# Layer 2 of a fused attention and MLP kernel: differences on another engine, sums in PSUM chains, attention at other times

## The chip, the cores and the metric

One core of a Trainium2 chip runs the whole program. The metric is the device time of one execution in microseconds (us). A profile is one separate execution, recorded instruction by instruction. The engines are TensorE (PE; its weight loads are listed apart as PEld), VectorE (DVE), ScalarE (ACT) and GpSimd (POOL); SyncE (SP) issues the DMAs. Each runs its instructions in the order in which they stand.

## The reference, cut to what matters

Attention with a per-head decay `lam`, then an MLP. q, k, v are (4, 8, 768, 64), in 12 blocks of 64; the MLP is 512 to 2048 to 512 over 3072 tokens, all float32.

```python
for b in range(nb):                       # 12 blocks of 64
    intra = einsum('bhic,bhjc->bhij', qb, kb) * Dmask      # Dmask[i, j] = lam ** (i - j), i >= j
    intra = einsum('bhij,bhjd->bhid', intra, vb)
    inter = einsum('bhid,bhde->bhie', qb * lam_pow, kv_state)
    out[:, :, sl] = intra + inter
    kv_state = lam_block * kv_state + einsum('bhsd,bhse->bhde', kb * rev_pow, vb)
h = x @ w_in                              # x: the attention's output, tokens x 512
g = maximum(h, 0) + log1p(exp(-abs(h)))   # softplus
return g @ w_out
```

## The kernel before, in words

Every float32 matrix product of the MLP is three float32r products: an operand is split in a high half (a rounding copy on ScalarE) and a low half (a subtraction on VectorE), and high x high, high x low and low x high are summed in PSUM. The 3072 tokens are six chunks of 512 (4 batch rows x 128 positions).

- Chunks 0 and 1 run a plain ("classic") MLP. For each of 16 blocks of 128 hidden rows there are 12 matmuls of layer 1 (`mlp1`, into a PSUM bank `h`), a softplus (`chain_act`), the split (`chain_hi`, `chain_lo`) and 12 matmuls of layer 2 (`mlp2`, into four banks `o`). There are two `h` banks; attention's output `z` uses them as well.
- Chunks 2 and 3 (group q=1) and chunks 4 and 5 (q=2) run with 7 block products in place of 8 (a Strassen-Winograd scheme) in both layers. Layer 1 (`l1`) makes four blocks 11, 12, 21, 22 of the softplus in SBUF. Layer 2 (`l2`, n = 0 to 6, each n four pieces jp, each piece 12 matmuls) needs differences of these blocks: `l2_minus` makes them in place on GpSimd, 16 instructions of 128x1024 in each group. `l2_split` splits a piece into the tile `gb`, `l2_products` multiplies it with the weights `wb`, `l2_end` takes a finished product out of PSUM into the sums U, P, V, R, and `l2_store` writes a block of 512 x 256 to HBM.
- The weight sums for the 7 products are made on GpSimd beside the classic stage (`prepare`: tiles `cs`, split into `sk`, stored to HBM as `w1d` and `w2d`).
- Attention of chunk c is four units g (`burst`: `outs` of one unit and `scores` of the next on TensorE; masks, decays and states on VectorE and ScalarE), put between the MLP's matmuls. `x_copy` takes `z` out of PSUM, `x_minus` and `x_block` make the seven split operands `xb` of layer 1.

From classic block 16 of the sequence on, the order is made at build time by `Plan`: each operation has an engine, an assumed duration, its buffers and a due time. Where several could start on an engine, the earliest due goes first. On the chip only the resulting order on each engine holds, with semaphores for data and buffers. 22 slots `b8` of 8 KB in a partition hold the loads and the split operands.

Lines used below: `chain_act` 589, `chain_hi` 593, `chain_lo` 597, `mlp1` 608, `mlp2` 622, `outs` 509, `scores` 478 and 482, `prepare` 866 to 898, `load_unit` 916, keys' decay 926, masks 946, copy of a state 955, query decay 971, `x_copy` 981, `x_block` 993 and 996, `x_minus` 1004, `l1_products` 1075, `l1_sum` 1122, `l2_minus` 1190, `l2_split` 1199 and 1202, `l2_products` 1217, `l2_end` 1235 and 1237, `l2_store` 1247.

Of the kernel before, what the change touches and what calls it, by code (L numbers as in the profile page):

```python
# [18 lines left out]
NP = H // 2  # L19
# [4 lines left out]
LAG = 4  # L24


class Plan:
# [57 lines left out]
    def order(self):  # L85
# [25 lines left out]
        while done < len(ops):  # L111
# [81 lines left out]
def decay_attention_softplus_ffn(  # L193
# [660 lines left out]
    def prepare(which, j):  # L854
        e, o = 2 * j, 2 * j + 1
        pairs = [divmod(w_order.index((f, which)), 2) for f in (e, o)]
        due = clock
# [34 lines left out]
        add("DVE", dve(1024), lo, [*four, (*sk, 0)], [(*sk, 1)], due=due + 7)  # L892
# [18 lines left out]
    def load_unit(g, due):  # L911
        if g < 2 * NP + 2:
            return

        def load():
            nc.sync.dma_start(out=unit(g), in_=att[g // NP, g % NP])

        add("SP", 0.06, load, [], u_keys(g, "q", "k0", "k1", "kt2", "kt3", "v"), [("b8", ("U", g))], size=1.05, due=due, behind=bursts.get(g - 2))
# [22 lines left out]
    def after_scores(g, due):  # L941
# [25 lines left out]
        for n, r in ((1, hi), (0, lo)):  # L967
# [4 lines left out]
            add("DVE", 0.69, decay, [("t", g)], u_keys(g, "q"), due=due)  # L972
# [14 lines left out]
    def x_block(q, n, c, p, due):  # L987
# [11 lines left out]
        add("DVE", dve(1024), low, [*of, (*key, 0)], [(*key, 1)], due=due)  # L999

    def x_minus(q, to, x, y, due):
# [52 lines left out]
    def l1_load(q, j):  # L1054
        for n, (a, b) in enumerate(((0, 4), (4, 7))):
            def load(n=n, a=a, b=b):
# [4 lines left out]
                due=clock - 7, behind=l1_ops.get((q, j - 2) if j > 1 else (q, -1)),  # L1061
# [126 lines left out]
    def l2_minus(q, jp, to, x, y, due):  # L1188
        def minus():
            nc.gpsimd.tensor_sub(out=l_pair(q, to, jp), in0=l_pair(q, x, jp), in1=l_pair(q, y, jp))  # L1190
        add("POOL", pool(1024), minus, lks(q, x, jp) + lks(q, y, jp), lks(q, to, jp), due=due)

    def l2_split(q, n, jp):
        blk = blocks[n]
# [9 lines left out]
        add("ACT", act(1024), high, lks(q, blk, jp), [(*key, 0)], [("b8", key)], due=clock - 4, behind=l2_ops[-4] if len(l2_ops) > 3 else l1_ops[q, 6])  # L1204
        add("DVE", dve(1024), low, [*lks(q, blk, jp), (*key, 0)], [(*key, 1)], due=clock - 2)

    def l2_products(q, n, jp):
        key = ("G2", q, n, jp)

        def run():  # L1210
            if jp == 0:
                E2[q, n] = [obank(f"e{q}_{n}_{m}") for m in range(2)]
            w = W2[q, n, jp // 2]
            for k in range(2):
                for m in range(2):
                    for r, (a, b) in enumerate(((0, 0), (1, 0), (0, 1))):
                        nc.tensor.matmul(  # L1217
                            E2[q, n][m], lhsT=w[:, 2 * (jp % 2) + k, a, m * 128 : (m + 1) * 128], rhs=G2[key][:, b, k],
                            start=jp == 0 and k == 0 and r == 0, stop=jp == 3 and k == 1 and r == 2,
                        )  # L1220

        return ffn(
            R12, run, [(*key, 0), (*key, 1), ("W2", q, n, jp // 2, 0)], [("E2", q, n, m, 0) for m in range(2)],
            [("o", ("E2", q, n, m)) for m in range(2)] if jp == 0 else (),
        )

    def l2_end(q, name, n, of=None, op=ALU.add, due=1.0):

        for m in range(2):
            def run(m=m):  # L1230
                if name not in OB or OB[name][0] != q:
                    OB[name] = q, t4([128, 2, 512], F32, f"{name}{q}")
                to = OB[name][1][:, m]
                if of is None:
                    nc.scalar.copy(out=to, in_=E2[q, n][m])
                else:
                    nc.vector.tensor_tensor(out=to, in0=OB[of][1][:, m], in1=E2[q, n][m], op=op)  # L1237
            key = ("OB", q, name)
            add(
                "ACT" if of is None else "DVE", 0.69, run,  # L1240
                [("E2", q, n, m, 0), *([] if of is None else [("OB", q, of, m)])], [(*key, m)],
                [("b4", key)] if m == 0 and of != name else (), due=clock + due,
            )

    def l2_store(q, name, c, dh):
        def run():
            nc.sync.dma_start(
                out=out[c, dh * 256 : (dh + 1) * 256].rearrange("(m q) i -> q m i", m=2), in_=OB[name][1]
            )
# [121 lines left out]
```

## Time and profile before

| | |
|---|---|
| Time, median of 3 runs | 568.33 us (567.51 to 569.15) |
| Time of the profiled execution | 567.39 us |
| Its span, first to last instruction | 565.6 us |
| TensorE busy | 549.1 us (97%) |
| VectorE busy | 426.5 us (75%) |
| ScalarE busy | 288.7 us (51%) |
| GpSimd busy | 215.8 us (38%) |

A row of the timeline gives the start, the time from the start of the first to the end of the last instruction of its run, engine, line, operation, output<-inputs, shape and count; in square brackets is the idle time ahead of it and who ended it. A row of waits gives the sum, the number and the longest. Matmuls are pipelined: one 128x512 matmul is listed at 393 ns, while a run of them advances by 227 ns each, so runs are read by their starts. The MLP of the classic chunks fills the first 226 us, group 1 the stretch to 409 us, group 2 the rest; layer 2 of group 1 starts at 316.7 us, that of group 2 at 485.1 us.

### The profile page before, as it was taken

Reading aid. Unit: us, or ns where it says so; the run is one execution under the profiler, and the core shown is the slowest. Engines: PE = TensorE matmul, PEld = TensorE weight load, DVE = VectorE, ACT = ScalarE, POOL = GpSimd, SP = SyncE. Lnnn points to the kernel's source line nnn. Section 1 sums busy time; section 2 is a strip of 40 time slices with the busy share of each in tenths; the row PEclk is TensorE's granted clock in tenths of the full one; section 3 lists DMA queues with packets and bytes.
Section 4 is the critical chain, followed back from the end, with each engine's and each line's share of the span. In section 5 each row is a group of like instructions: output and inputs, shape, how many; then the busy total and the mean of one; then the engine's idle time right before and its main releaser. Section 6 shows DMA issues by size and latency. Waiting matters only on the chain. (4 is left out here: it accounts for less than half of the span.)

```text
span 565.6 us, 10346 instructions
## 1 busy us (share of the span) xinstructions
PE 549.1 (97%) x4275; PEld 449.6 (79%) x4275; DVE 426.5 (75%) x498; ACT 288.7 (51%) x420; POOL 215.8 (38%) x138
## 2 busy tenths in 40 slices
PE   8999999999999999799999999998999999999996
PEld 6888888888888878578788878876888888888885
DVE  8999999969267678985666999999533336779763
ACT  5998975475445456545446653355023234474300
POOL 1000000475445468675440979920000006869100
PEclk9999999999999999999999999999999999999999
DMA  8999699838734449279966957462798332528502
GB/s 309 399 407 407 232 373 368 279 150 280 280 149 149 150 159 378 116 269 349 403 203 229 374 220 261 149 225 75 270 412 339 131 124 100 222 90 319 224 0 111
DMA packets 37919, 136.97 MB, mean 242 GB/s; under 512 B 3186, under 2 KB 11378, under 8 KB 29042
## 3 DMA queue, kind: packets, MB, share of 16 engines
q1 hardware_dynamic: 37872, 136.33, 64.8%
q8 instruction: 33, 0.54, 0.4%
q14 instruction: 12, 0.10, 0.0%
q10 hardware_dynamic: 2, 0.00, 0.0%
HBM read 100.66 MB, written 35.65 MB: 241 GB/s over the span
## 5 line engine op out<-in xcount | busy, mean ns | idle before, releaser
L1217 PE MATMUL e<-gb,wb 128*128 128x512 f32 x672 | 156.4, 393 | 2.8 <-DVE gb L1202 2.8
L1190 POOL TENSOR_TENSOR l<-l,l 128x1024 f32<-128x1024 f32 x32 | 104.2, 3281 | 126.2 <-DVE gb L1202 125.6
L1217 PEld LDWEIGHTS e<-gb,wb 128*128 128x128 f32 x672 | 126.7, 189 | 30.3 <-DVE gb L1202 3.6
L866 POOL TENSOR_TENSOR cs<-w 128x512 f32<-128x512 f32 x32 | 48.4, 1534 | 180.3 <-PE h L608 105.3
L1202 DVE TENSOR_TENSOR gb<-l,gb 128x1024 fp32r<-128x1024 f32 x56 | 97.3, 1774 | 6.7 <-ACT gb L1199 6.6
L608 PE MATMUL h<-x,w 128*128 128x512 f32 x384 | 92.2, 392 | 1.3 <-ACT xs L981 1.3
L622 PE MATMUL o<-w,g 128*128 128x512 f32 x384 | 92.4, 392 | 0.0
L608 PEld LDWEIGHTS h<-x,w 128*128 128x128 f32 x384 | 71.5, 188 | 16.8 <-ACT xs L981 1.5
L622 PEld LDWEIGHTS o<-w,g 128*128 128x128 f32 x384 | 71.5, 188 | 15.2
L1075 PE MATMUL B<-xb,wa 128*128 128x512 f32 x288 | 71.9, 392 | 3.9 <-DVE xb L996 2.6
L1199 ACT CAST gb<-l 128x1024 fp32r<-128x1024 f32 x56 | 56.5, 1049 | 26.4 <-PE e L1217 10.1
L1075 PEld LDWEIGHTS B<-xb,wa 128*128 128x128 f32 x288 | 53.6, 188 | 16.5 <-DVE xb L996 3.4
L880 POOL TENSOR_TENSOR cs<-cs 128x256 f32<-128x256 f32 x64 | 61.8, 980 | 2.5
L1104 ACT ACTIVATE l<-l 128x512 f32<-128x512 f32 x48 | 30.2, 631 | 44.6 <-DVE l L1122 44.5
L1075 PE MATMUL D<-xb,wa 128*128 128x512 f32 x192 | 49.0, 391 | 0.0
L1075 PE MATMUL A<-xb,wa 128*128 128x512 f32 x192 | 48.9, 390 | 0.0
L597 DVE TENSOR_TENSOR g<-l,g 128x512 fp32r<-128x512 f32 x32 | 28.8, 899 | 17.6 <-ACT g L593 17.3
L1075 PEld LDWEIGHTS A<-xb,wa 128*128 128x128 f32 x192 | 35.9, 188 | 7.7 <-DMA wa<-w1d 0.2
L1075 PEld LDWEIGHTS D<-xb,wa 128*128 128x128 f32 x192 | 35.9, 188 | 7.5
L589 ACT ACTIVATE l<-h 128x512 f32<-128x512 f32 x32 | 19.1, 597 | 36.1 <-PE h L608 28.7
L971 DVE TENSOR_TENSOR att<-att,lp 64x512 f32<-64x512 f32 x32 | 31.6, 989 | 0.5
L926 ACT ACTIVATE att<-att,rp 64x256 f32<-64x256 f32 x56 | 27.9, 505 | 7.2 <-DMA att<-in_att 6.5
(111 smaller groups left out, 621.9 us busy)
## 6 DMA issues: line engine op xcount, KB each, us to landing
wb<-w2d SPq DMA_DIRECT2D x28, 1024.0 KB, 5.7
att<-in_att SPq DMA_DIRECT2D x17, 1024.0 KB, 7.3
raw<-in_wts SPq DMA_DIRECT2D x32, 512.0 KB, 10.1
wa<-w1d SPq DMA_DIRECT2D x16, 1024.0 KB, 8.1
wa<-w1d SPq DMA_DIRECT2D x16, 768.0 KB, 9.2
w1d<-sk SPq DMA_DIRECT2D x8, 1024.0 KB, 4.8
w2d<-sk SPq DMA_DIRECT2D x8, 1024.0 KB, 5.5
w2d<-w SPq DMA_DIRECT2D x24, 256.0 KB, 4.4
```

The costliest lines, as they stand in the source:

```text
L597: nc.vector.tensor_sub(out=g[:, 1, :], in0=l_tiles.pop(s), in1=g[:, 0, :])
L608: nc.tensor.matmul(h_tiles[s], lhsT=w[:, i, cs], rhs=x[:, j, :], start=p == 0 and n == 0, stop=p == NP - 1 and n == 2,)
L622: nc.tensor.matmul(o_tiles[c][b], lhsT=g[:, i, b * 128 : (b + 1) * 128], rhs=w[:, j], start=f == 0 and n == 0, stop=f == NF - 1 and n == 2,)
L866: nc.gpsimd.tensor_add(out=T8[cs][:, 2 * n : 2 * n + 2].rearrange("q h e -> q (h e)"), in0=w[:, 0], in1=w[:, 1])
L880: nc.gpsimd.tensor_tensor(out=t[:, to], in0=t[:, x], in1=t[:, y], op=op)
L971: nc.vector.tensor_mul(out=q, in0=q, in1=w[r])
L1075: nc.tensor.matmul(AB[q, j, to], lhsT=w[:, a, k * 128 : (k + 1) * 128], rhs=x[:, b, k], start=start and k == 0 and m == 0, stop=k == 1 and ...
L1104: nc.scalar.activation(l, l if of is None else AB[(q, j, of)], AF.Softplus)
L1190: nc.gpsimd.tensor_sub(out=l_pair(q, to, jp), in0=l_pair(q, x, jp), in1=l_pair(q, y, jp))
L1199: nc.scalar.copy(out=G2[key][:, 0], in_=l_pair(q, blk, jp))
L1202: nc.vector.tensor_sub(out=G2[key][:, 1], in0=l_pair(q, blk, jp), in1=G2[key][:, 0])
L1217: nc.tensor.matmul(E2[q, n][m], lhsT=w[:, 2 * (jp % 2) + k, a, m * 128 : (m + 1) * 128], rhs=G2[key][:, b, k], start=jp == 0 and k == 0 an ...
```

## The change

- Layer 2's differences are made on VectorE (`nc.vector.tensor_sub`), and block 11 is changed twice in place of 22; the products run in the order of the table `order2`.
- Products that belong to one sum stay in PSUM: products 0 and 1 add up in the banks X, 4 and 2 in Y, and 5, 3 and 6 in X2 (`chains`). The sums are taken out when a chain or a prefix of it is done (`sums`): 10 VectorE additions and 4 ScalarE copies in a group, for 18 and 2. Each piece's 12 matmuls are two operations of 6, one for each half m of the output rows; each half is stored by itself (256 KB), eight stores in a group for four. `stores` names the output block of each.
- In the planned part the classic softplus is written in place into its PSUM bank, and both halves of the split read it there; the bank is free after the low half.
- The due times become a table `LEAD`: copies of `z` are due 20 us earlier, weight sums 2.7 us (w_in) and 5.6 us (w_out) earlier, splits 7 us earlier, attention's bursts start at other times and distances.

```diff
-            nc.gpsimd.tensor_sub(out=l_pair(q, to, jp), in0=l_pair(q, x, jp), in1=l_pair(q, y, jp))
-        add("POOL", pool(1024), minus, lks(q, x, jp) + lks(q, y, jp), lks(q, to, jp), due=due)
+            nc.vector.tensor_sub(out=l_pair(q, to, jp), in0=l_pair(q, x, jp), in1=l_pair(q, y, jp))
+        add("DVE", dve(1024), minus, lks(q, x, jp) + lks(q, y, jp), lks(q, to, jp), due=due, kind="two")
...
+        def soften():
+            l_tiles[s] = h_tiles.pop(s)
+            nc.scalar.activation(l_tiles[s], l_tiles[s], AF.Softplus)
+        add("ACT", 0.6, soften, [], [("h", s)], due=due)
+        add("ACT", 0.62, lambda: chain_hi(s), [("h", s)], [("g", s, 0)], [("b4", ("g", s))], due=due)
+        add("DVE", 0.69, lambda: chain_lo(s), [("h", s), ("g", s, 0)], [("g", s, 1), ("g", s)], due=due)
...
-    blocks = ("11", "21", "22", "12", "11", "22", "21")
+    order2 = ((0, "11"), (4, "11"), (1, "21"), (2, "22"), (5, "11"), (3, "12"), (6, "21"))
...
+    chains = {0: "X", 4: "Y", 1: "X", 2: "Y", 5: "X2", 3: "X2", 6: "X2"}
...
+        begins = w_n in (0, 4, 5)
+                    nc.tensor.matmul(
+                        E2[q, to, m], lhsT=w[:, 2 * (jp % 2) + k, a, m * 128 : (m + 1) * 128], rhs=G2[key][:, b, k],
+                        start=begins and jp == 0 and k == 0 and r == 0, stop=jp == 3 and k == 1 and r == 2,
...
+            nc.sync.dma_start(out=out[c, dh * 256 + m * 128 : dh * 256 + (m + 1) * 128], in_=OB[q, name][:, m])
+        add("SP", 0.06, run, [("OB", q, name, m)], [], size=0.262, due=clock + 3)
+    sums = {0: [("U", "X", None)], 4: [("D", "Y", "U")], 1: [("P", "X", None)], 2: [], 5: [("V", "X2", "U"), ("V", "Y", "V")], 3: [("D", "X2", "D")], 6: [("U", "X2", "U")]}
+    stores = {1: ("P", 0, 0), 5: ("V", 1, 0), 3: ("D", 1, 1), 6: ("U", 0, 1)}
...
-            attention(3, [clock + 7.5 * n for n in range(5)])
+            attention(3, [clock + LEAD["att3"] + LEAD["step3"] * n for n in range(5)])
...
-                attention(2 * q + 3, [clock + 10 * n for n in range(5)])
+                attention(2 * q + 3, [clock + LEAD["att5"] + LEAD["step5"] * n for n in range(5)])
```

VectorE in layer 2 of group 1 (gb1_n_jp: the split of piece jp of the n-th product; l1_11, l1_21, l1_22: blocks of the softplus; U1, P1, D1: sums; att20: an attention unit), before:

```order
L1202 TENSOR_TENSOR gb1_1_3_3479<-l1_21_1_3192,gb1_1_3_3479 128x1024
L1202 TENSOR_TENSOR gb1_2_0_3517<-l1_22_0_2628,gb1_2_0_3517 128x1024
L1202 TENSOR_TENSOR gb1_2_1_3534<-l1_22_0_2628,gb1_2_1_3534 128x1024
L1202 TENSOR_TENSOR gb1_2_2_3554<-l1_22_1_3062,gb1_2_2_3554 128x1024
L1237 TENSOR_TENSOR P1_3600<-U1_3475,e1_1_0_3481 128x512
L1237 TENSOR_TENSOR P1_3600<-U1_3475,e1_1_1_3482 128x512
L1202 TENSOR_TENSOR gb1_2_3_3602<-l1_22_1_3062,gb1_2_3_3602 128x1024
```

The same part of VectorE's order now:

```order
L1210 TENSOR_TENSOR gb1_2_3_3460<-l1_21_1_3054,gb1_2_3_3460 128x1024
L1198 TENSOR_TENSOR l1_11_0_2617<-l1_22_0_2628,l1_11_0_2617 128x1024
L1249 TENSOR_TENSOR D1_3485<-e1_Y_0_3414,U1_3412 128x512
L1210 TENSOR_TENSOR gb1_3_0_3476<-l1_22_0_2628,gb1_3_0_3476 128x1024
L1249 TENSOR_TENSOR D1_3485<-e1_Y_1_3426,U1_3412 128x512
L1210 TENSOR_TENSOR gb1_3_1_3496<-l1_22_0_2628,gb1_3_1_3496 128x1024
```

The differences (L1198) now stand among the splits; they were in GpSimd's order before.

ScalarE late in the classic stage (att14: the unit whose scores w14 are next; z12, z13: attention outputs in `h` banks; h28 to h30, l30: classic blocks; sk: weight sums), before:

```order
L885 CAST sk1_2_2169<-cs1_2_2168 128x4x256
L955 COPY att14_2094<-st_14_1795 64x512
L981 COPY xs3_2278<-z12_2096 128x512
L981 COPY xs3_2278<-z13_2215 128x512
L589 ACTIVATE l30_2317<-h30_2282 128x512
```

The same part now:

```order
L963 COPY att13_1893<-st_13_1595 64x512
L989 COPY xs3_2151<-z12_2078 128x512
L835 ACTIVATE h28_2129<-h28_2129 128x512
L598 CAST g28_2174<-h28_2129 128x512
L1001 CAST xb1_1_2179<-xs2_1656 128x1024
L893 CAST sk0_4_2147<-cs0_4_2146 128x4x256
L934 ACTIVATE att14_2169<-att14_2169,rp1_110 64x4x64 x4
L835 ACTIVATE h29_2182<-h29_2182 128x512
L598 CAST g29_2269<-h29_2182 128x512
L989 COPY xs3_2151<-z13_2219 128x512
L963 COPY att14_2169<-st_14_1774 64x512
L835 ACTIVATE h30_2272<-h30_2272 128x512
```

The copies of z12 and z13 moved ahead of att14's copy; a weight sum and att14's key decays stand ahead of h29.

TensorE's last matmuls (e2_6_m and e2_X2_m: the two halves m of the last sum), before:

```order
L1217 MATMUL e2_6_1_5037<-gb2_6_2_5033,wb2_6_1_5018 128x512 x3
L1217 MATMUL e2_6_0_5036<-gb2_6_3_5051,wb2_6_1_5018 128x512 x3
L1217 MATMUL e2_6_1_5037<-gb2_6_3_5051,wb2_6_1_5018 128x512 x3
L1217 MATMUL e2_6_0_5036<-gb2_6_3_5051,wb2_6_1_5018 128x512 x3
L1217 MATMUL e2_6_1_5037<-gb2_6_3_5051,wb2_6_1_5018 128x512 x3
```

And now:

```order
L1229 MATMUL e2_X2_1_4889<-gb2_6_1_4930,wb2_6_0_4928 128x512 x6
L1229 MATMUL e2_X2_0_4881<-gb2_6_2_4947,wb2_6_1_4965 128x512 x6
L1229 MATMUL e2_X2_1_4889<-gb2_6_2_4947,wb2_6_1_4965 128x512 x6
L1229 MATMUL e2_X2_0_4881<-gb2_6_3_4967,wb2_6_1_4965 128x512 x6
L1229 MATMUL e2_X2_1_4889<-gb2_6_3_4967,wb2_6_1_4965 128x512 x6
```

Half 0 is done 6 matmuls ahead of the end, where it was done 3 ahead.

## Rows read from the trace of the kernel before

**Rows 1.** The page: busy time, share of the span, instructions of each engine

```profile
PE 549.1 (97%) x4275; PEld 449.6 (79%) x4275; DVE 426.5 (75%) x498; ACT 288.7 (51%) x420; POOL 215.8 (38%) x138
```

**Rows 2.** Waits of PE: who waited for whom, us, times, longest

```profile
PE e L1217 <- DVE gb L1202: 2.8, 2, 2.3
PE B L1075 <- DVE xb L996: 2.6, 2, 2.1
PE h L608 <- ACT xs L981: 1.3, 1, 1.3
...
PE B L1075 <- ACT xb L993: 1.1, 1, 1.1
...
PE z L509 <- DVE att L971: 1.0, 1, 1.0
```

**Rows 3.** Windows: length, PE, PEld, DVE, ACT, POOL busy (count), PE clock, DMA

```profile
394.00:398.00 4.00, 4.00 (x11) 3.14 (x12) 3.82 (x4) 0.00 (x0) 0.00 (x0) 0.57 0.00 0
```

**Rows 4.** Chain that ended last: start us, us, engine, tile, line, count

```profile
316.67 2.75 PE e L1217 x12
...
393.87 15.05 PE e L1217 x58
...
485.08 75.49 PE e L1217 x333
...
560.60 1.37 DVE U L1237 x2
```

**Rows 5.** Timeline of DVE, and then POOL, in layer 2 of group 1

```profile
321.36 9.73 DVE L1202 TENSOR_TENSOR gb<-l,gb 128x1024 fp32r<-128x1024 f32 x3 [0.28 <-ACT gb L1199]
...
347.50 1.41 DVE L946 TENSOR_TENSOR att<-w,mask 64x512 f32<-64x512 f32 x2
...
375.33 0.69 DVE L971 TENSOR_TENSOR att<-att,lp 64x512 f32<-64x512 f32 x1
...
378.86 3.48 DVE L1202 TENSOR_TENSOR gb<-l,gb 128x1024 fp32r<-128x1024 f32 x3
...
339.13 31.61 POOL L1190 TENSOR_TENSOR l<-l,l 128x1024 f32<-128x1024 f32 x8 [2.96 <-DVE gb L1202]
```

**Rows 6.** Groups by line: count, busy us, mean ns, idle before

```profile
L1190 POOL TENSOR_TENSOR l<-l,l 128x1024 f32<-128x1024 f32 x32 | 104.2, 3281 | 126.2 <-DVE gb L1202 125.6
L1202 DVE TENSOR_TENSOR gb<-l,gb 128x1024 fp32r<-128x1024 f32 x56 | 97.3, 1774 | 6.7 <-ACT gb L1199 6.6
```

**Rows 7.** Timeline of ACT at the end of the classic stage

```profile
201.27 0.62 ACT L955 COPY att<-st 64x512 f32<-64x512 f32 x1 [2.17 <-PE w L482]
201.90 1.07 ACT L981 COPY xs<-z 128x512 f32<-128x512 f32 x2
```

**Rows 8.** Timeline of PE, ACT, DVE and POOL where layer 1 of group 1 begins

```profile
218.79 1.15 PE L509 MATMUL z<-att 128*64 128x64 f32 x32
...
221.20 0.59 ACT L981 COPY xs<-z 128x512 f32<-128x512 f32 x1
...
221.81 2.13 DVE L1004 TENSOR_TENSOR xs<-xs 128x1024 f32<-128x1024 f32 x1 [1.35 <-ACT xs L981]
...
230.73 1.21 DVE L996 TENSOR_TENSOR xb<-xs,xb 128x1024 fp32r<-128x1024 f32 x1
...
222.94 5.66 POOL L880 TENSOR_TENSOR cs<-cs 128x256 f32<-128x256 f32 x4
```

**Rows 9.** Timeline of ACT, DVE and PE around classic block 20

```profile
137.71 0.60 ACT L589 ACTIVATE l<-h 128x512 f32<-128x512 f32 x1 [2.60 <-PE h L608]
138.34 0.62 ACT L593 CAST g<-l 128x512 fp32r<-128x512 f32 x1
...
139.78 0.68 DVE L597 TENSOR_TENSOR g<-l,g 128x512 fp32r<-128x512 f32 x1
...
140.23 2.88 PE L608 MATMUL h<-x,w 128*128 128x512 f32 x12
```

**Rows 10.** Line 916, the loads of attention's units

```profile
DMA to landing us min/median/max: 4.7/7.5/11.5
```

More of the change, by code (lines that the diff above doesn't have):

```diff
@@ L856, in prepare @@
         pairs = [divmod(w_order.index((f, which)), 2) for f in (e, o)]
-        due = clock
+        due = clock + LEAD["prepare"] + which * LEAD["prepare2"]
         tag = f"{which}_{j}"
@@ L891, in prepare @@
         prepared.append(len(plan.ops))
-        add("DVE", dve(1024), lo, [*four, (*sk, 0)], [(*sk, 1)], due=due + 7)
+        add("DVE", dve(1024), lo, [*four, (*sk, 0)], [(*sk, 1)], due=due + 7, kind="two")
         if which == 0:
@@ L971, in decay @@
                 nc.vector.tensor_mul(out=q, in0=q, in1=w[r])
-            add("DVE", 0.69, decay, [("t", g)], u_keys(g, "q"), due=due)
+            add("DVE", 0.69, decay, [("t", g)], u_keys(g, "q"), due=due, kind="two")
     def x_copy(g, due):
@@ L998, in x_block @@
         add("ACT", act(1024), high, of, [(*key, 0)], [("b8", key)], due=due)
-        add("DVE", dve(1024), low, [*of, (*key, 0)], [(*key, 1)], due=due)
+        add("DVE", dve(1024), low, [*of, (*key, 0)], [(*key, 1)], due=due, kind="two")
     def x_minus(q, to, x, y, due):
@@ L1202, in low @@
             nc.vector.tensor_sub(out=G2[key][:, 1], in0=l_pair(q, blk, jp), in1=G2[key][:, 0])
-        add("ACT", act(1024), high, lks(q, blk, jp), [(*key, 0)], [("b8", key)], due=clock - 4, behind=l2_ops[-4] if len(l2_ops) > 3 else l1_ops[q, 6])
-        add("DVE", dve(1024), low, [*lks(q, blk, jp), (*key, 0)], [(*key, 1)], due=clock - 2)
-    def l2_products(q, n, jp):
+        add("ACT", act(1024), high, lks(q, blk, jp), [(*key, 0)], [("b8", key)], due=clock - LEAD["split"], behind=l2_ops[-LEAD["split_depth"]] if len(l2_ops) >= LEAD["split_depth"] else l1_ops[q, LEAD["split_from"]])
@@ L1208, in l2_products @@
+        add("DVE", dve(1024), low, [*lks(q, blk, jp), (*key, 0)], [(*key, 1)], kind="two", due=clock - LEAD["split"] + 2)
+    chains = {0: "X", 4: "Y", 1: "X", 2: "Y", 5: "X2", 3: "X2", 6: "X2"}
+    def l2_products(q, n, jp, m):
         key = ("G2", q, n, jp)
+        w_n = order2[n][0]
+        to = chains[w_n]
+        begins = w_n in (0, 4, 5)
         def run():
-            if jp == 0:
-                E2[q, n] = [obank(f"e{q}_{n}_{m}") for m in range(2)]
+            if jp == 0 and begins:
+                E2[q, to, m] = obank(f"e{q}_{to}_{m}")
@@ L1245, in l2_store, with l2_end @@
[L1245 to L1250 removed]
+            R6, run, [(*key, 0), (*key, 1), ("W2", q, n, jp // 2, 0)], [("E2", q, to, m)],
+            [("o", ("E2", q, to, m))] if jp == 0 and begins else (),
+        )
+    def l2_end(q, name, chain_, m, of=None, ahead=1.0):
+        def run():
+            if (q, name) not in OB:
+                OB[q, name] = t4([128, 2, 512], F32, f"{name}{q}")
+            to = OB[q, name][:, m]
+            if of is None:
+                nc.scalar.copy(out=to, in_=E2[q, chain_, m])
+            else:
+                nc.vector.tensor_add(out=to, in0=E2[q, chain_, m], in1=OB[q, of][:, m])
+        key = ("OB", q, name)
+        add(
+            "ACT" if of is None else "DVE", 0.6 if of is None else 0.69, run,
+            [("E2", q, chain_, m), *([] if of is None else [("OB", q, of, m)])], [(*key, m)],
+            [("b4", key)] if m == 0 and of != name else (), due=clock + ahead,
+        )
@@ L1318, in decay_attention_softplus_ffn @@
             if q < NCH // 2 - 1 and j == 0:
-                attention(2 * q + 2, [clock + 14 * n for n in range(5)])
+                attention(2 * q + 2, [clock + LEAD["att4"] + LEAD["step4"] * n for n in range(5)])
         for n in range(7):
```

106 lines of the change are left out of this document (36 added, 70 removed).

## The prediction, on record before the changed kernel ran

> **What bounds the kernel now.** I read the page's first part, then TensorE's waits, then the windows around the longest of them, then the other engines' timelines there. TensorE is busy for 549.1 of 565.6 us [rows 1], so work taken off another engine gives time back only where TensorE stands and waits for it. The change leaves every matmul in place, with its shape. What can be won is therefore a short list: TensorE's waits once the planned part runs, the time lost after a wait at a lower clock, and the end.
>
> The waits add up to 8.8 us [rows 2], apart from those of the start, which the change doesn't touch. The reader is to see where they are: 2.8 us for the split `gb` and 1.0 for an attention decay are in layer 2 of group 1, where VectorE has no idle time to speak of; 1.3 us is classic block 30, waiting for a copy of `z`; 2.6 and 1.1 us are the start of layer 1 of group 1, waiting for the operand `xb`. Group 2 has none: 333 matmuls run there in 75.49 us, 0.2267 us each [rows 4].
>
> [...]
>
> **Layer 2's differences on VectorE.** GpSimd's 32 instructions of 3.28 us [rows 6] go and 32 of VectorE come. The price is read where GpSimd is idle: three splits of the same form in 3.48 us, 1.16 each [rows 5]. While GpSimd works they take 3.24 each (9.73 for three), and 1.77 on the mean of all 56 [rows 5, 6]. A mask multiplication that reads PSUM keeps to 0.70 in the middle of GpSimd's run (1.41 for two) [rows 5], so it is the instructions with two SBUF inputs that are held up.
>
> [...]
>
> In layer 2 of group 1 VectorE then has 28 splits and 16 differences at 1.16, 51.0 us; 10 additions at 0.68 (1.37 for two [rows 4]), 6.8; five attention blocks of 3.5 us (375.33 to 378.86 [rows 5]), 17.7; and 11 differences and splits of `xs` at 1.16, 12.8: 88.3 us. TensorE has from 316.67 to 393.87 + 15.05 = 408.92 us [rows 4], 92.25 us, less the waits 3.8 and the clock's 1.9: 86.5 us. So VectorE is as loaded as TensorE. But six of these instructions (7.0 us) now stand ahead of layer 2's first matmul, in a part of layer 1 where VectorE has room, which leaves 81.3. By the order each split then comes 5 us or more ahead of its matmuls; closest is the last operand of group 2's layer 1, about 2 us ahead. The 3.8 us of waits and the 1.9 us of clock go: 5.7 us. Bounds: nothing gained if VectorE is slowed by something else than GpSimd (a rival below), and no gain above 5.7.
>
> In group 2, 44 x 1.16 + 6.8 = 58 us of VectorE stand against 76 of TensorE. Nothing waits there before, nor after.
>
> **Chains in PSUM.** Eight VectorE additions fewer and two ScalarE copies more in each group are counted above. The matmuls alternate by runs of 6 for 3, in four banks as before; layer 1 runs by 6 too. No price.
>
> **The end.** Today two additions, 1.37 us, follow the last matmul [rows 4], and then a store of 512 KB; the span ends at 565.6, 3.6 us after the second addition. Now half 0 is ready 6 matmuls (1.36 us) before the end, so one addition of 0.68 and a store of 256 KB are left. The addition saves 0.7. The smaller store saves between 0 (all of the 3.6 fixed) and 1.8 (none of it); I take 0.6, nearer to the fixed cost, since the store is alone at the end. Together 1.3.
>
> **Classic softplus in PSUM, copies of z.** Block 30 waits because the copies of two `z` (1.07 us) stand behind a copy that waits 2.2 us for the next scores [rows 7]. Now they stand ahead of it: 1.3 us go. In exchange an `h` bank is free only after both halves of the split, 1.3 us later than now (the softplus is 0.60; the halves add 0.62 and 0.68 [rows 9]). The tightest place is block 21, which takes block 20's bank: softplus from 137.71, low half 139.78 to 140.46, and block 21 starts at 140.23 [rows 9]. VectorE reaches that low half some 0.5 us earlier now, since block 19's no longer meets GpSimd; a wait of 0 to 0.5 us remains. A softplus written to PSUM isn't in the trace; one that reads PSUM takes 0.60 [rows 9], and I take the same.
>
> **Earlier weight sums and attention.** `prepare` moves up, and its VectorE halves stand ahead of low halves that free a bank (ahead of h29's, for one), behind GpSimd's sums and, on ScalarE, behind key decays that wait for a load. SP takes some attention loads later in its queue: unit 11 behind two weight stores. A unit's load lands 4.7 to 11.5 us after its issue, 7.5 on the median [rows 10]; in the order I find 1 to 3 us of room at a median load (units 14, 18 and 23), so a slow one costs up to 2.5 each. For all of this and block 21 together: 0 to 5 us; I take 1.7.
>
> **Layer 1's start.** After the last `z` of chunk 3 (218.79 + 1.15) comes its copy, done at 221.79, then VectorE's chain from 221.81 to 231.94 [rows 8]. TensorE is 3.2 us late for it, and 0.5 once more for the last operand. Now the copy is due earlier, but behind four key decays and a weight sum on ScalarE: the chain starts 0 to 1.1 us sooner, and GpSimd is still beside it. The 0.5 should go, since that operand moved up. I take 2.3 us left of 3.7, so 1.4 saved; bounds 0 and 3.7.
>
> **Sum.** 5.7 + 1.3 + 1.3 + 1.4 - 1.7 = 8.0 us saved. The profiled execution took 567.39, which gives 559.4; the median of the runs is 0.94 above that execution, so 560.3. I say 560.2.
>
> **Rivals.**
> 1. *The start of layer 1 comes free as well and nothing new waits.* The copy of `z` and the chain would have to gain 3 us; for it speaks the earlier due time, against it GpSimd's sums beside the chain [rows 8]. 560.2 - 1.7 - 2.3 = 556.2.
> 2. *Banks and loads take the gain back.* Held 1.3 us longer, `h` banks make TensorE wait where one is reused at once, at four places or so (5.2 us more than I count); low halves behind late weight sums do the same. For it: block 21's room of nearly nothing [rows 9] and loads up to 11.5 us [rows 10]. Against: most reuses have 5 us or more. 560.2 + 5.2 = 565.4.
> 3. *VectorE becomes the bound in layer 2 of group 1* (slower than before). If the differences and splits stayed at 1.77 us [rows 6] with GpSimd idle, 44 x 0.61 = 26.8 us come on top; VectorE would need 81.3 + 26.8 = 108.1 against 86.5, 21.6 late. Gone too would be the 5.7: 568.3 - 2.3 + 21.6 = 587.6. From a mean of about 1.45 us on (room of 5.2 plus the gain of 8.1, over 44) the change loses. Against it: 1.16 with GpSimd idle [rows 5].
>
> **How the numbers follow.** Forecast 0.66 (its own range 557.5 to 563.5, from the bounds 0 to 5 of the new waits and 0 to 3.7 at layer 1's start), rival 1 0.10, rival 2 0.16, rival 3 0.08. The range 556.3 to 565.2 takes in the first, nearly all of rival 1 and half of rival 2. A measurement here can tell 0.3%, 1.7 us: faster means below 566.6. Forecast, rival 1 and two thirds of rival 2 lie there: 0.87. Within 0.3% lies the rest of rival 2: 0.05. Slower is rival 3: 0.08.
>
> **What would show it right or wrong.** In layer 2 VectorE's `gb` and difference rows should be near 1.16 us, TensorE's list of waits should hold no `gb` line, and no window should show a clock below 1.00 between 300 and 420 us. The line for `xb` should stay, at 2 to 3 us. After the last matmul one addition of 0.68 should stand. GpSimd should end near 290 us. It would be wrong if new lines appear: `h` waiting for VectorE's split (the held banks), scores waiting for ScalarE's key decay or a load (late units), `gb` waiting at more than 1.3 us an instruction (rival 3).

## The result and the profile after

The changed kernel takes 560.50 us (median of 4 runs, 558.73 to 561.86) against 568.74 us (567.51 to 570.11) in the same comparison: ratio 0.9853, interval 0.9816 to 0.9889. Measured a second time it took 560.42 us (558.85 to 560.85), ratio 0.9841, interval 0.9819 to 0.9863. The forecast was 560.2.

The page's first line of the kernel after, and then its list of TensorE's waits from 20 to 560 us (us, times, longest), answer to [rows 1, 2]:

```profile
PE 549.3 (98%) x4275; PEld 450.9 (81%) x4275; DVE 412.6 (74%) x514; ACT 291.4 (52%) x424; POOL 109.7 (20%) x106
```

```profile
PE B L1083 <- DVE xb L1004: 2.5, 1, 2.5
PE z L514 <- DVE att L979: 0.9, 1, 0.9
PE B L1083 <- DVE l L1130: 0.5, 1, 0.5
```

TensorE does the same work. The lines for `gb` and `h` are gone, that for `xb` stayed. The attention decay that TensorE waits for is another one (at 218.97 us, where it was at 378.99), and the wait of 0.5 for a sum of layer 1 is new. GpSimd lost its half, and VectorE is less busy than before although 32 instructions came to it and only 16 short ones left: the differences no longer hold up its splits, which take 1.22 us on the mean of all 56 for 1.77 [rows 6]. The groups by line from 310 to 410 us (count, busy us, mean ns, idle before) and VectorE's timeline in layer 2 of group 1 answer to [rows 5, 6]:

```profile
L1210 DVE TENSOR_TENSOR gb<-l,gb 128x1024 fp32r<-128x1024 f32 x27 | 32.4, 1218 | 1.7 <-ACT gb L1207 1.7
L1198 DVE TENSOR_TENSOR l<-l,l 128x1024 f32<-128x1024 f32 x16 | 19.2, 1217 | 0.0
```

```profile
326.69 4.65 DVE L1210 TENSOR_TENSOR gb<-l,gb 128x1024 fp32r<-128x1024 f32 x4
...
341.00 2.35 DVE L1198 TENSOR_TENSOR l<-l,l 128x1024 f32<-128x1024 f32 x2
```

One instruction is listed at 1.22 us; four in a row take 4.65, 1.16 each, the price of the prediction.

Where the time went is read from the starts of the stages' first matmuls, in the profiled executions (us):

| stretch | before | after | second profile of after |
|---|---|---|---|
| to group 1's layer 1 | 225.44 | 225.51 | 225.38 |
| group 1, layer 1 | 91.07 | 91.28 | 90.49 |
| group 1, layer 2 | 92.25 | 87.14 | 87.12 |
| group 2, layer 1 | 76.16 | 76.16 | 76.16 |
| group 2, layer 2, to the end of the span | 80.68 | 80.01 | 79.95 |

One attention output `z` (32 matmuls, 1.08 us) moved from layer 1 to layer 2 of group 1: 128 of them stood in each stretch, now 96 and 160. Like for like, layer 2 of group 1 gained 6.2 us and layer 1 lost 1.3 (0.5 in the second profile).

The loss is at layer 1's start. Windows of the kernel after (length, busy us and count of PE, PEld, DVE, ACT, POOL, granted clock, DMA share, GB/s), with the whole of 300 to 400 us for [rows 3]:

```profile
230.00:232.00 2.00, 0.67 (x2) 0.57 (x3) 2.00 (x3) 0.76 (x2) 0.64 (x1) 0.66 0.01 4
232.00:234.00 2.00, 2.00 (x6) 1.58 (x5) 2.00 (x5) 0.41 (x1) 2.00 (x2) 0.50 0.31 121
234.00:236.00 2.00, 2.00 (x6) 1.55 (x5) 0.39 (x1) 0.64 (x1) 1.92 (x3) 0.50 1.02 384
236.00:238.00 2.00, 2.00 (x7) 1.52 (x7) 2.00 (x2) 0.00 (x0) 1.92 (x3) 0.63 1.05 298
...
300.00:400.00 100.00, 100.00 (x832) 82.33 (x831) 89.10 (x102) 54.01 (x70) 0.00 (x0) 1.00 0.62 232
```

In layer 2 of group 1 TensorE is busy all the time, at a granted clock of 1.00. At layer 1's start the granted clock was 0.50 in the windows from 232 to 236 us, and 0.66 and 0.63 in those beside them. The timelines of PE, DVE and POOL there answer to [rows 8]:

```profile
231.34 2.07 PE L1083 MATMUL B<-xb,wa 128*128 128x512 f32 x4 [2.54 <-DVE xb L1004]
233.21 2.76 PE L1083 MATMUL D<-xb,wa 128*128 128x512 f32 x6
235.77 2.34 PE L1083 MATMUL A<-xb,wa 128*128 128x512 f32 x6
237.95 1.55 PE L1083 MATMUL B<-xb,wa 128*128 128x512 f32 x6
...
221.07 2.31 DVE L1012 TENSOR_TENSOR xs<-xs 128x1024 f32<-128x1024 f32 x1
...
230.07 1.21 DVE L1004 TENSOR_TENSOR xb<-xs,xb 128x1024 fp32r<-128x1024 f32 x1
...
222.25 6.81 POOL L888 TENSOR_TENSOR cs<-cs 128x256 f32<-128x256 f32 x4
```

The chain starts 0.7 us sooner than before (221.07 for 221.81), and TensorE's last wait there ends 0.7 sooner. But the 16 matmuls behind it take 6.61 us (231.34 to 237.95), where the wait for the same operand in the trace of before, 2.07 us, was followed by 16 in 3.78.

ScalarE at the end of the classic stage, answering to [rows 7]: the copy of `z` now stands ahead of the copy that waits for scores.

```profile
200.50 0.59 ACT L989 COPY xs<-z 128x512 f32<-128x512 f32 x1 [1.61 <-PE z L514]
201.62 0.62 ACT L963 COPY att<-st 64x512 f32<-64x512 f32 x1 [0.53 <-PE w L487]
```

The end, answering to [rows 4], in the timelines of PE, DVE and the queue of SP:

```profile
544.69 11.72 PE L1229 MATMUL e_X<-gb,wb 128*128 128x512 f32 x51
...
556.45 0.69 DVE L1249 TENSOR_TENSOR U<-e_X,U 128x512 f32<-128x512 f32 x1 [0.67 <-PE e_X L1229]
...
555.81 1.69 SPq L1259 DMA_DIRECT2D out_dram<-U  x2
```

The last matmul ends at 556.41, one addition follows until 557.14, and the span ends at 560.1, 2.96 us after the addition.

### The profile page after: what moved, and what is told of

Read it like the earlier page. It is cut to its first block, busy times and chain, and to the rows that moved or that the text cites. A ratio compares the mean times of both kernels' runs of the same rounds, so it can differ in the third digit from the quotient of the medians.

```text
span 560.1 us, 10331 instructions
## 1 busy us (share of the span) xinstructions
PE 549.3 (98%) x4275; PEld 450.9 (81%) x4275; DVE 412.6 (74%) x514; ACT 291.4 (52%) x424; POOL 109.7 (20%) x106
## 4 chain that ended last, share of the span: by engine, by line
PE 89%; DVE 5%; DMA 3%; POOL 1%; issue 1%; ACT 0%; SPq 0%; POOLq 0%
PE e_X L1229 20%; PE h L613 15%; PE o L627 13%; PE B L1083 12%; PE e_Y L1229 8%; PE D L1083 8%; PE A L1083 7%; PE z L514 3%; DMA att<-in_att 3%; PE w L483 2%; DVE xs L1012 1%; POOL cs L888 1%; DVE sk L896 1%; DVE xb L1004 1%; DVE att L979 1%
## 5 line engine op out<-in xcount | busy, mean ns | idle before, releaser
L1229 PE MATMUL e_X<-gb,wb 128*128 128x512 f32 x480 | 111.0, 390 | 0.0
L1229 PEld LDWEIGHTS e_X<-gb,wb 128*128 128x128 f32 x480 | 89.8, 188 | 18.9
L1207 ACT CAST gb<-l 128x1024 fp32r<-128x1024 f32 x56 | 57.9, 1052 | 35.6 <-PE e_Y L1229 17.7
L1210 DVE TENSOR_TENSOR gb<-l,gb 128x1024 fp32r<-128x1024 f32 x56 | 67.1, 1218 | 6.5 <-ACT gb L1207 6.3
L888 POOL TENSOR_TENSOR cs<-cs 128x256 f32<-128x256 f32 x64 | 60.6, 961 | 2.5
L1229 PE MATMUL e_Y<-gb,wb 128*128 128x512 f32 x192 | 44.5, 390 | 0.0
L1229 PEld LDWEIGHTS e_Y<-gb,wb 128*128 128x128 f32 x192 | 36.0, 188 | 7.5
L1198 DVE TENSOR_TENSOR l<-l,l 128x1024 f32<-128x1024 f32 x32 | 38.5, 1217 | 0.0
L896 DVE TENSOR_TENSOR sk<-cs,sk 128x1024 fp32r<-128x1024 f32 x16 | 21.8, 1363 | 8.9 <-ACT sk L893 8.9
```

The source lines that it names most:

```text
L888: nc.gpsimd.tensor_tensor(out=t[:, to], in0=t[:, x], in1=t[:, y], op=op)
L896: nc.vector.tensor_sub(out=T8[sk][:, :, 1], in0=T8[cs][:, 4:8], in1=T8[sk][:, :, 0])
L1198: nc.vector.tensor_sub(out=l_pair(q, to, jp), in0=l_pair(q, x, jp), in1=l_pair(q, y, jp))
L1207: nc.scalar.copy(out=G2[key][:, 0], in_=l_pair(q, blk, jp))
L1210: nc.vector.tensor_sub(out=G2[key][:, 1], in0=l_pair(q, blk, jp), in1=G2[key][:, 0])
L1229: nc.tensor.matmul(E2[q, to, m], lhsT=w[:, 2 * (jp % 2) + k, a, m * 128 : (m + 1) * 128], rhs=G2[key][:, b, k], start=begins and jp == 0 a ...
```

## The experiments

**The engine of the differences alone.** The order of every other engine is that of the changed kernel.

```diff
-            nc.vector.tensor_sub(out=l_pair(q, to, jp), in0=l_pair(q, x, jp), in1=l_pair(q, y, jp))
+            nc.gpsimd.tensor_sub(out=l_pair(q, to, jp), in0=l_pair(q, x, jp), in1=l_pair(q, y, jp))
```

> The changed kernel with the 32 differences of layer 2 back on GpSimd, each instruction of every engine in the same order as in the changed kernel. Theory A (the gain of 5.7 us in layer 2 of group 1 comes from GpSimd no longer standing beside VectorE's two-input instructions): the splits go from 1.22 us back to about 1.8 us each, a difference takes 3.3 us instead of 1.2, lines for gb come back among TensorE's waits (4 us or more, and lost clock behind them); time 565 to 570 us. Rival B (the new order of operands and dues in layer 2 brought the gain by itself, the engine of the differences doesn't matter): no gb line, 560 to 561.5 us.

569.47 us (568.83 to 571.93, 10 runs), ratio 1.0023 (1.0008 to 1.0037): 9.0 above the changed kernel, all of its gain. Its groups by line, and two of TensorE's waits:

```profile
L1210 DVE TENSOR_TENSOR gb<-l,gb 128x1024 fp32r<-128x1024 f32 x56 | 118.1, 2150 | 4.0 <-ACT gb L1207 3.7
...
L1198 POOL TENSOR_TENSOR l<-l,l 128x1024 f32<-128x1024 f32 x32 | 102.5, 3226 | 153.9 <-DVE gb L1210 152.7 <-issue 1.2
```

```profile
PE z L514 <- DVE att L979: 3.1, 3, 1.8
...
PE B L1083 <- DVE l L1130: 1.9, 1, 1.9
```

The same splits take 2.15 us on the mean in place of 1.22. The time is the one that theory A expected, but no line for `gb` came back: what TensorE waits for behind the slower splits is VectorE's attention work, and a sum in group 2's layer 1. In its profile layer 2 of group 1 is 4.7 us longer than in the changed kernel's (91.82 for 87.14) and group 2, which had no wait before, 4.0 longer (2.8 in layer 1, 1.2 in layer 2). The new order doesn't bear the differences on GpSimd.

**The same edit in the kernel before**, with its old products, sums and times:

```diff
-            nc.gpsimd.tensor_sub(out=l_pair(q, to, jp), in0=l_pair(q, x, jp), in1=l_pair(q, y, jp))
-        add("POOL", pool(1024), minus, ...
+            nc.vector.tensor_sub(out=l_pair(q, to, jp), in0=l_pair(q, x, jp), in1=l_pair(q, y, jp))
+        add("DVE", dve(1024), minus, ...
```

> The kernel before with one edit: its 32 differences of layer 2 on VectorE, in its old order of operands and with all its old times; TensorE's order stays as it was. Theory A: the splits fall from 1.77 to about 1.2 us, the 3.8 us of waits in layer 2 of group 1 and the 1.9 us of clock behind them go, the wait for the copy of z, the start of layer 1 and the end stay: 568.7 - 5.7 = 563.0 us. Rival B (the order, not the engine): VectorE gets 16 more instructions in a stretch where it had no idle time, the gb waits stay or grow: 568 us or more.

571.30 us (569.59 to 573.40), ratio 1.0037 (1.0018 to 1.0055): theory A was wrong, and rival B's time came. Timelines of DVE and PE:

```profile
381.55 2.35 DVE L996 TENSOR_TENSOR xb<-xs,xb 128x1024 fp32r<-128x1024 f32 x2
...
390.09 1.22 DVE L1202 TENSOR_TENSOR gb<-l,gb 128x1024 fp32r<-128x1024 f32 x1
...
232.11 1.19 PE L1075 MATMUL B<-xb,wa 128*128 128x512 f32 x4 [2.07 <-DVE xb L996]
233.13 2.56 PE L1075 MATMUL D<-xb,wa 128*128 128x512 f32 x6
235.50 2.13 PE L1075 MATMUL A<-xb,wa 128*128 128x512 f32 x6
237.47 1.53 PE L1075 MATMUL B<-xb,wa 128*128 128x512 f32 x6
...
391.36 21.62 PE L1217 MATMUL e<-gb,wb 128*128 128x512 f32 x82 [5.51 <-DVE gb L1202]
```

Each instruction is cheap here too, 1.22 us a split and 1.21 a difference on the mean from 310 to 410 us: VectorE is busy for 425.2 us with 32 instructions more than in the kernel before, where it was 426.5. But in the old order eight instructions of group 2's chain of `xs` and `xb`, from 380.40 on, stand ahead of the split that TensorE needs at 385.9. I read this as a wait by order, not by load; no run moved that split ahead to show it. In the old order the cheap engine doesn't pay. The order of the products, the chains in PSUM with their fewer additions and the earlier splits came together in the change and weren't tried apart, so it isn't shown which of them it needs.

**The old times in the changed kernel** (attention, copies of `z` and weight sums due as before):

```diff
-LEAD = {..., "x": -18.3, ..., "prepare": -2.7, "prepare2": -2.9, "att2": -2.0, ..., "step4": 22.9, "att5": 10.8, ...
+LEAD = {..., "x": 2.0, ..., "prepare": 0.0, "prepare2": 0.0, "att2": 0.0, ..., "step4": 14, "att5": 0.0, ...
```

> The changed kernel with the old due times of attention, of the copies of z and of the weight sums (differences on VectorE, chains in PSUM and softplus in PSUM stay). Theory A (as predicted: the new times save 1.3 us at the copy of z and about 1.2 us at layer 1's start, and cost 1.4 us of new waits): an h<-xs wait of about 1.3 us comes back, the two waits of 0.9 and 0.5 us go; 560.5 to 563 us. Rival C (the new times matter more than that, since with the differences on VectorE layer 2 has no room for attention blocks where they stood): gb or attention waits in layer 2 of group 1 and 565 us or more.

577.13 us (575.61 to 578.43), ratio 1.0144 (1.0123 to 1.0164), far beyond theory A. The time lies in rival C's range, but not by its mechanism: layer 2 of group 1 took 86.73 us there and held one wait of 0.7. The chain of waits at layer 1's start:

```profile
225.42 1.06 ACT sk L893
...
226.50 1.40 DVE sk L896
...
227.93 9.86 DMA w1d<-sk
...
237.86 1.05 ACT xb L1001
...
238.94 1.71 DVE xb L1004
...
240.69 2.08 PE B L1083 x4
```

The operand `xb` waits for the buffer of a late weight sum, and that for the sum's store: TensorE stands still for 10.9 us. The new engine without the new order loses, and so do the new order and engine without the new times. These times are needed in layer 1, not in layer 2.

**The order of the chain at layer 1's start** (two VectorE instructions behind the operand that is late):

```diff
+                plan.moves += [(d, x5), (x6, x5)]
```

> The changed kernel with two VectorE instructions at the start of layer 1 of group 1 (the low half of xb 6 and the difference of xs for xb 3) moved behind the low half of xb 5, for which TensorE waits 2.5 us; nothing else moves. Theory D (the wait is due to these two, 3.5 us, standing ahead): the wait falls below 0.6 us and the 3.0 us of lost clock behind it go; but the operand xb 3, whose ScalarE half waits for a buffer of the weight sums, is then late by 0.5 to 3 us; 555 to 558.5 us. Rival E (VectorE's chain beside GpSimd is the bound, in whatever order): a wait of the same 2.5 us appears at the next operand; 560.5 us.

561.77 us (561.28 to 562.29), ratio 0.9874 (0.9857 to 0.9890). TensorE's waits:

```profile
PE z L519 <- DVE att L984: 3.4, 2, 2.5
PE B L1090 <- DVE uv L1137: 1.5, 1, 1.5
PE B L1090 <- DVE xb L1009: 0.7, 1, 0.7
```

The wait for `xb` went from 2.5 to 0.7, and what stands further back in VectorE's queue became late instead: a sum of layer 1 (1.5) and an attention decay (2.5; the other 0.9 of its line is the wait that the changed kernel has too). There was no gain. The wait came back as rival E had it, in two pieces and later than at the next operand.

**GpSimd out of the way at layer 1's start.** Two of the weight blocks are summed in their first 16 columns only, so their sums are left out.

```diff
+            few = 16 if tag in ("1_4", "0_6") else 512
             nc.gpsimd.tensor_add(
-                ..., in0=w[:, 0], in1=w[:, 1]
+                ...[:, :few], in0=w[:, 0, :few], in1=w[:, 1, :few]
```

> The changed kernel with the twelve GpSimd sums of two weight blocks, those that stand beside the start of layer 1 of group 1 (218 to 239 us), cut to 16 columns; the two blocks' split on ScalarE and VectorE stays in size and place but takes other data, so these two blocks' sums are left out of the result. Every engine's order stays. Theory F (VectorE's chain there is late because GpSimd stands beside it, and the last operand because its buffer waits for the second block's sums): VectorE's two-input instructions between 219 and 240 us fall from 1.5 to 2.3 us to about 1.2, the wait of 2.5 us for xb 5 and the 3.0 us of clock behind it go: 555 to 557.5 us. Rival G (it is the order and the late copy of z that set it, not GpSimd): the wait stays above 2 us, 560 us or more.

555.88 us (555.53 to 555.98), ratio 0.9777 (0.9762 to 0.9791). VectorE's and TensorE's timelines:

```profile
220.75 1.24 DVE L1021 TENSOR_TENSOR xs<-xs 128x1024 f32<-128x1024 f32 x1
...
227.16 1.23 DVE L1013 TENSOR_TENSOR xb<-xs,xb 128x1024 fp32r<-128x1024 f32 x1
...
228.68 1.09 PE L1092 MATMUL B<-xb,wa 128*128 128x512 f32 x4
229.61 1.52 PE L1092 MATMUL D<-xb,wa 128*128 128x512 f32 x6
```

The first difference falls from 2.31 to 1.24, the split that was late starts at 227.16 for 230.07, and TensorE no longer waits for it. In both kernels VectorE runs the same instructions in the same order without idle time from 219.6 us to the end of that split: 8.8 us here, 11.7 in the changed kernel. So it is their length beside GpSimd that makes the split late, and not a wait of VectorE's own. Layer 1's start still costs the changed kernel 4.6 us, with the clock behind the wait.

**GpSimd put back beside layer 2**, without giving it the differences: 32 added subtractions whose output nobody reads.

```diff
+                for n in range(2):
+                    nc.gpsimd.tensor_sub(out=idle, in0=l_pair(q, to, jp)[:, n], in1=...)
```

> The changed kernel with 32 added GpSimd instructions in layer 2 of group 1 (128x512, two SBUF inputs, 1.5 us each when alone; two behind each of VectorE's 16 differences, their result is used by nobody). All other engines keep their order. Theory A (what decides is GpSimd beside VectorE): differences and splits there go from 1.22 to 1.6 us or more, VectorE (89 us busy of the 100 from 300 to 400) becomes the bound, gb waits come back; 564 to 578 us; group 2 keeps 1.22. Rival B (GpSimd's old instructions mattered only because their own results came late): 1.22 stays, 560.5 us.

577.10 us (576.16 to 578.96), ratio 1.0155 (1.0131 to 1.0179), 16.6 above the changed kernel. VectorE's groups from 310 to 410 us:

```profile
L1214 DVE TENSOR_TENSOR gb<-l,gb 128x1024 fp32r<-128x1024 f32 x26 | 38.6, 1506 | 6.5 <-ACT gb L1211 6.5
L1199 DVE TENSOR_TENSOR l<-l,l 128x1024 f32<-128x1024 f32 x16 | 23.0, 1454 | 0.0
L979 DVE TENSOR_TENSOR att<-att,lp 64x512 f32<-64x512 f32 x10 | 12.1, 1211 | 0.2
L954 DVE TENSOR_TENSOR att<-w,mask 64x512 f32<-64x512 f32 x10 | 6.9, 688 | 0.3
```

The differences and splits rise from 1.22 us to 1.45 and 1.51 here. In group 2, from 410 to 490 us, where GpSimd is idle, nothing of the kind shows: VectorE's 48 instructions take 36.92 us, 0.77 each, and the changed kernel's 51 take 39.94, 0.78 each. The decays, with two SBUF inputs, rise from 0.68 to 1.21 us, the masks, which read PSUM, stay at 0.69. So in these rows, as in [rows 5], it is the instructions with two SBUF inputs that take longer beside GpSimd. No `gb` line came back here either: TensorE waits for VectorE's masks and decays, 9.6 and 4.0 us.

**Softplus to SBUF again**, the rest as changed:

```diff
-            l_tiles[s] = h_tiles.pop(s)
-            nc.scalar.activation(l_tiles[s], l_tiles[s], AF.Softplus)
+            chain_act(s)
```

> The changed kernel with the classic part's softplus written to one SBUF buffer again, as before the change; every engine's order stays. Theory H (as predicted: softplus in PSUM is no gain, it only holds the banks 1.3 us longer without a wait behind it): 560.0 to 561.0 us, no h line among TensorE's waits in either. Rival I (the single SBUF buffer was a brake: a softplus must wait until VectorE has read the one before): ScalarE's softplus shows waits for VectorE's low half, and h or o waits appear; over 562 us.

562.02 us (561.36 to 562.20), ratio 0.9882 (0.9864 to 0.9900), 1.5 above the changed kernel. Layer 1 of group 1 starts at the same time (225.35), so holding the banks longer cost nothing in the classic stage, and nothing was won there by it. The loss is later, in layer 1 of group 1 (91.81 us for 91.28 and 90.49 in the changed kernel's two profiles), in a list of other small waits (2.7 for `xb`, 1.3 for `z`, 0.5 and 0.3). Neither theory has it: it is more than H allowed, and there is no `h` or `o` wait. Every engine's order is that of the changed kernel. What differs on VectorE are the classic low halves: 16 of them have both inputs in SBUF again, where those of the changed kernel read PSUM and take 0.69 us, and from 20 to 200 us VectorE is busy for 147.77 us with 191 instructions, for 145.52 with as many. The prediction had this side of the softplus in PSUM for one block alone (block 19, 0.5 us). How the small waits come of it wasn't traced.

**The last two stores as one:**

```diff
-            if w_n in stores:
+            if w_n in stores and not (q == 2 and w_n == 6):
...
+                nc.sync.dma_start(out=out[c, 256:512].rearrange("(m q) i -> q m i", m=2), in_=OB[q, "U"])
```

> The changed kernel with the last two stores of 256 KB joined to one of 512 KB behind both additions, as before the change; nothing else moves. Theory J (as predicted): the time from the last addition to the end grows by 0.6 us; 561.1 us. Bounds: 0 (the end is a fixed cost) and 1.8 us (it grows with the size). Both stay within 562.3 us.

561.53 us (560.95 to 563.04), ratio 0.9881 (0.9861 to 0.9901). In its profile the last addition ends at 555.00 and the span at 559.2, 4.2 us later, where the changed kernel needs 2.96. The smaller store is worth about 1.2 us against this form, and 0.67 against that of the kernel before (3.63).

**The changed kernel again**, for its spread:

> The changed kernel itself, unedited, beside the next one on one chip. Every theory expects 560.5 us, between 558.7 and 561.9 as in its four runs so far; the wait for xb 5 at layer 1's start stays at 2.5 us, and what the clock costs behind it may differ from run to run.

560.42 us, as told above. Its waits are the same at layer 1's start (2.54 for `xb`), but the 16 matmuls behind it take 5.29 us (231.20 to 236.49) for 6.61. The four executions had mean granted clocks of 0.997, three times, with 560.23 to 560.85 us, and 1.000 with 558.85.

**The sums later, nothing left out.** The GpSimd sums beside layer 1's start are held back until the late operand is done.

```diff
+MOVES = [("0_6 whole 0", "x1_5 low"), ("0_6 whole 1", "0_6 whole 0"), ("1_4 sum 4", "0_6 whole 1"), ...
...
+                nc.gpsimd.tensor_sub(out=idle[:, :16], in0=x, in1=x)
```

> The changed kernel with GpSimd held back at the start of layer 1 of group 1 and nothing left out: after the first two sums of weight block 1_4, a 16-column GpSimd instruction that reads the low half of xb 5 holds its queue, then come the two first sums of block 0_6, the four others of 1_4 and the four others of 0_6; the two blocks' splits and stores and the sums of block 1_5 move behind layer 1's own instructions. Theory F (GpSimd beside VectorE makes the chain late): VectorE's instructions from 222 to 228 us take 1.2 us, the wait for xb 5 falls from 2.5 to 0.5 us or less, the lost clock goes, xb 3 gets an earlier buffer: 555.5 to 558 us, below both kernels. Rival K (the work only moves: the late sums now hold up the attention or layer 1's sums between 235 and 250 us): waits of 2 us or more come up there, 559 to 562 us.

565.42 us (564.45 to 566.02), ratio 0.9934 (0.9915 to 0.9953). TensorE's waits, and VectorE's timeline where the longest is:

```profile
PE B L1096 <- DVE l L1143: 5.8, 1, 5.8
PE B L1096 <- DVE xb L1016: 0.9, 1, 0.9
```

```profile
253.89 1.23 DVE L907 TENSOR_TENSOR sk<-cs,sk 128x1024 fp32r<-128x1024 f32 x1 [5.74 <-ACT sk L904]
255.15 0.69 DVE L1143 TENSOR_TENSOR l<-B,d 128x512 f32<-128x512 f32 x1
```

The wait at the start falls to 0.9 and comes back, longer, 25 us later, behind the stretch that rival K named; the time is above both ranges. A weight sum's split stands in VectorE's order ahead of a sum that TensorE needs, and its input is late now. This is the second rival's mechanism, low halves behind late weight sums, in another place.

**Room at layer 1's start by VectorE alone.** GpSimd is left; one difference goes behind the late operand, copies of `o` go to ScalarE, and two key decays and two other instructions go later.

```diff
+MOVES = [("xs(2, 2)", "x1_5 low"), ("decay 16 1", "sum 1 0 22"), ("0_6 low", "decay 16 0"), ...
...
-                (nc.vector.tensor_copy if b % 2 else nc.scalar.copy)(...)
+                (nc.vector.tensor_copy if b % 2 and c == 0 else nc.scalar.copy)(...)
```

> The changed kernel with GpSimd left as it is, but less ahead of xb 5 on VectorE at layer 1's start: only the difference of xs for xb 3 moves behind the low half of xb 5 (its ScalarE half has to wait for a buffer anyway), the two copies of the second chunk's output go from VectorE to ScalarE, two key decays on ScalarE move behind the high half of xb 5, and two short reorderings behind it (layer 1's sum ahead of a query decay, a query decay ahead of a weight split). Theory D' (part of the wait is order): xb 5 comes 1.8 to 2.4 us earlier, its wait falls to 0.7 us or less and no clock is lost behind it; unit 16's output may then wait up to 1.3 us; 557 to 559.5 us, against 560.4 for the changed kernel. Rival E (VectorE's total beside GpSimd is the bound, whatever the order): the wait comes back behind xb 5, as with two instructions moved; 560.5 to 562 us.

559.05 us (558.29 to 560.23), ratio 0.9817 (0.9792 to 0.9841). TensorE's timeline:

```profile
230.22 1.19 PE L1093 MATMUL B<-xb,wa 128*128 128x512 f32 x4 [1.37 <-DVE xb L1013]
231.25 1.53 PE L1093 MATMUL D<-xb,wa 128*128 128x512 f32 x6
232.61 1.52 PE L1093 MATMUL A<-xb,wa 128*128 128x512 f32 x6
```

The wait is 1.2 us shorter, though not the 0.7 or less of theory D', and after it the clock stays up (on the mean 0.999 to 1.000 in all five executions). The time is within that theory's range. The median is the lowest of a kernel that computes everything, but the interval overlaps that of the changed kernel, so the 1.4 us between them are likely, not certain.

## Why the prediction came out

**Layer 2 of group 1: right.** 5.7 us were forecast, with no gain above that; like for like it is 6.2 (92.25 + 1.08 - 87.14). The steps stand one by one: 1.16 us an instruction, no `gb` wait, no clock below 1.00 there. Of the 5.7, 1.9 were the clock behind the 2.3 us wait for `gb`: 58 matmuls took 15.05 us [rows 3, 4], where at group 2's pace, 75.49 us for 333, they would take 13.15. After, the granted clock is 1.00 from 300 to 420 us. The engine alone, put back, costs 9.0, of which 4.7 lie in this stage, and GpSimd's presence with 32 smaller instructions costs 16.6. Where the 0.5 beyond the forecast lie isn't settled. GpSimd ended at 277 us, not near 290.

**Copy of `z`: right.** From the start of the `z` before block 30 to the block itself it was 3.58 us (198.96 to 202.54) and is 2.17 (199.31 to 201.48): 1.4 gained, 1.3 forecast.

**New waits: the size near, the kind not.** From block 30 to layer 1 the way is 1.1 us longer (22.90, now 24.03), where 1.7 was forecast, for banks, loads and key decays. No such line came. The one that came, 0.9, is VectorE's query decay at 218.23, behind the mask and the state of the same burst.

**The end: half.** 1.3 us were forecast and 0.67 came. The step that failed is "the addition saves 0.7". Before, the last matmul ended at 561.24 by TensorE's timeline (544.76 + 16.48), and of the two additions that [rows 4] show from 560.60 the first ran beside the last three matmuls. So one addition followed the last matmul then as now, ending 0.73 us after it both times. The row shows two; when its first starts must be held against the end of the matmuls. The store's 0.6 was right.

**Layer 1's start: the wait 0.7 longer than forecast, the clock left out.** "2.3 us left of 3.7" became 3.0 (2.54 and 0.50; 2.54 and 0.53 for a `z` in the second profile). The size that was missed is the clock behind the wait: I priced none, because the trace of before shows none after a wait of 2.07 there. The old order costs it too, in the profile of the second experiment: the same wait of 2.07 us, and then 5.36 us for the 16 matmuls (232.11 to 237.47) for 3.78. Against that profile's 92.71 us for the whole stretch (225.55 to 318.26) the changed kernel's second profile is 2.2 better, 1.1 without the moved `z`; 1.4 were forecast.

**Why the medians differ by more than the profiles.** The two profiled executions differ by 5.5 us (567.39 and 561.86), the medians by 8.2 and 8.6. Of the 43 other executions of the kernel before whose clock is on record, 7 had a mean granted clock of 0.996, with 567.8 us on the mean, as the profiled one had; 34 had 0.993 or 0.994, with 569.1, and 2 had 0.991, with 571.0. The changed kernel's eight: 1.000 (two, 558.7 and 558.9), 0.997 (five, 560.2 to 560.9) and 0.994 (one, the profiled one, 561.9). A step of 0.003 is 1.7 us at this length, about the 1.6 lost behind one such wait. So the profile of before was one of its best executions, and that of after its worst. That the other executions of before lost their clock at layer 1's start is inferred from these means and the second experiment's profile; no trace of them exists. The prediction's "0.94 above that execution" was too small an offset for before and of the wrong sign for after. It is by these that a sum of 8.0, of which the profiled pair shows 5.5, met the median. The mechanism in layer 2 and at the copy of `z` was right; that the whole sum came so near to the medians' 8.2 and 8.6 is in part luck, since the terms for the end and for layer 1's start were too large by the profiled pair, and the clock of the other executions made up for them.

**The rivals.** The forecast's own range, 557.5 to 563.5, is narrower than the two bounds that it names, which add up to 556.2 and 564.9; all medians of the changed kernel lie in either. The first rival wanted layer 1's start for nothing, 556.2: it came with GpSimd's sums cut there (555.88), not by the due times, as the prediction held against it. The second didn't come in the changed kernel. The third supposed slow instructions with GpSimd idle, and didn't come. With GpSimd put beside them their mean was 1.49 us, about the 1.45 from which the prediction let the change lose, and it lost. The prediction's sum gives 9.3 us late at this mean (44 x 0.33 - 5.2). But it holds a listed length against the 1.16 by which a run advances; against the listed 1.22 it is 6.7 (44 x 0.27 - 5.2). The 16.6 measured has the decays' 5.3 (10 x 0.53) besides and a clock of 0.93 from 310 to 410 us.

## What to carry to other kernels

Before moving work to an engine, read its price in rows where its neighbour is idle and where it works: here 1.16 against 1.77 to 2.15 us for the same instruction decided the change. Then look at what stands ahead of the moved work in its new queue: the same cheap instructions lost when the order was left, or the times. And a gain below 2 us isn't read from one pair of profiles (two executions of the changed kernel lie 3.1 us apart, 558.73 and 561.86): look at the clock of each before they are subtracted.

## What the runs showed of the hardware

The same wait in the same order, 2.07 us, was followed by 16 matmuls in 3.78 us in one execution, at a granted clock of 1.00 in every window from 232 to 240 us, and in another by 16 in 5.36 us, at 0.83 on the mean from 230 to 240 us. After 2.54 us they took 6.61 us, with 0.50 from 232 to 236 us, and 5.29, with 0.50 from 232 to 234. After 1.37 us the profiled execution lost none (1.00 in every window from 226 to 242 us), and by their mean clocks, 0.999 and 1.000, the four others didn't either. So a wait's price isn't its length: 2.5 us of idle time cost up to 2.9 more behind it, against the 3.75 that the 16 took in the last experiment.
